# An FFT followed by two mixture-of-experts layers: an expert's last block moved to second place, with branch hints for TensorE

## The chip, the cores and the metric

The kernel runs on one core of a Trainium2 chip. The metric is the device time of one execution in microseconds (us). The core has five instruction streams: PE (TensorE, matmuls), DVE (VectorE), ACT (ScalarE), POOL (GpSimd) and SP (SyncE, which only issues DMAs). Each has its own sequencer, which the profile lists apart: it evaluates branches, loads registers and waits for semaphores.

## The reference

```
X = rfft(x, axis=1);  y = irfft(X * F)                 # 8 x 3072 tokens, 256 channels
x = y.reshape(24576, 256)
# first MoE: 8 experts, top 1
e = argmax(x @ w_gate);  g = softmax(x @ w_gate)[e]
out = g * sigmoid(x @ w_output_gate)[e] * (relu(x @ w1[e]) @ w2[e])     # 256 -> 1024 -> 256
# second MoE, top 1 with capacity 768: an expert takes its first 768 tokens, the rest give 0
e2 = argmax(out @ v_gate);  out2 = softmax(...)[e2] * (relu(out @ v1[e2]) @ v2[e2])
```

## The kernel before

Only the first 86 tiles of 128 tokens are worked on in the first round (`ROUNDS`); a second round follows only where the second MoE's experts aren't full by then (`k.full`, L1863). The FFT stage writes each token's row, by an indirect DMA, into the DRAM buffer `xs` at its expert's rows. The first MoE then takes each expert's rows in blocks. The matrix products run in three passes on rounded halves: a high part `_h` and a low part `_l` of the rows, of the weights and of the hidden values.

A plain block (`block1`, L1093) has 256 rows. Its first layer is four `l1_pair`s of 12 matmuls (L821 to L823); after each, ACT makes `h_h` (L826) and DVE `h_l` (L827). DVE also computes the logits of the second MoE for the block before (L1040, 16 a block). Then `prep` (L844) transposes the next block's rows on TensorE (L865), ACT copies out the high part and DVE the low part (L872). The second layer `l2` (L831) is twice 24 matmuls (L837 to L839); ACT scales the result into `x2` (L1140) and POOL scatters the rows (L1002) and the logits (L1020). A wide block (`block_wide`, L917) has 384 rows, with a first layer of 48 longer matmuls (L929 to L931) and a second layer of 72.

An expert's rows are cut by `cut_blocks` (L432) into a number of plain blocks, `k.plain`, and one last block, wide or narrow (256 rows), as `k.wide` says, from row `k.first` on. All counts are read into registers on every engine at run time.

`moe1` (L1189) goes through the eight experts. At the start of an expert SP loads the next expert's block 0 into buffer `b0` or `b1`, this expert's block 1 into `a1` (`load_x(e, 1)`), and the last block's rows into `xb_f` (`load_last`, L893). `load_x` (L874) takes its row from the table `k.ahead`, which repeats the last block's start where a block isn't there. Then comes block 0, which after its first layer prepares block 1 into `xt` and, between the halves of its second layer, the last block into `xt_f` (L851, L857, L858). ACT and POOL split the next expert's weights beside it (`next_w`, L794, L809, L810). Blocks 1 to 7 stand in seven nested conditions, `If(nb > j)` (L1211 to L1218); block j loads block j + 1 into `a0`, `a1` or `a2` by turns and prepares it, whether it is there or not. A branch that isn't taken leaves the whole nest, and each engine then brings its semaphores to where they would be had it gone through. After the nest comes `last_block` (L906) with the condition on `wide` (L911), the wide arm first; both arms prepare the next expert's block 0.

Expert 0 is special: its first four blocks are run by `head` (L1171) in the arm `early` (L712) of `one_round`, if enough of its rows were there before the last scatters; `late()` is the other arm, behind it in the code. In this data expert 0 has four plain blocks, all in that arm. Experts 0, 1, 2 and 6 have a narrow last block, 3, 4, 5 and 7 a wide one. After expert 7, the index work of the second MoE runs beside its last block, and `tile_kernel` (L1720) branches on `k.known` (L1849) into two forms of the second MoE's first blocks, the usual one first.

Of the kernel before, what the change touches and what calls it, by code (L numbers as in the profile page):

```python
# [431 lines left out]
def cut_blocks(k):  # L432
# [13 lines left out]
    nc.vector.tensor_copy(k.plain, k.cntf)  # L446
    STT(out=k.cntf, in0=k.cntf, scalar=256.0, in1=n, op0=ALU.mult, op1=ALU.subtract)
# [16 lines left out]
def one_round(k, r, cap):  # L464
# [46 lines left out]
    for bi, b in enumerate(batches):  # L511
# [68 lines left out]
        for q in range(NQ + 2):  # L580
# [19 lines left out]
            if nb is None and q == 8 and len(batches) > 1:  # L600
# [4 lines left out]
                with tc.If(early > 0):  # L605
                    moe.load_x(0, 0, True)
        j0, j1 = span[b]
# [54 lines left out]
    def aheads():  # L662
# [21 lines left out]
        )  # L684
        nc.vector.tensor_copy(k.ahead, k.aheadf)

    work = [gate.chain_a2, gate.chain_b, counts, pads, aheads, lambda: cut_blocks(k)]
# [20 lines left out]

    if early is None:
        late()  # L710
    else:
        with tc.If(early > 0) as c:  # L712
            for j in range(1, EARLY):
                moe.load_x(0, j, True)
            weights()
            run(last[0])
            moe.prep(*moe.rows(0, 0))
            moe.head(0, [(0, 1)], last[1:])
            nc.sync.dma_start(out=moe.w2gb, in_=k.a["w2gb"])
            beside = [work[:0], work[:0], work[:2], work[2:4], work[4:5], work[5:]]  # L720
            moe.head(1, [(0, 2)], [lambda f=f: run(*f) for f in beside], True)
            for j in range(2, EARLY - 1):
                moe.head(j, [(0, j + 1)])
            ahead()
            moe.load_x(0, EARLY)
            moe.head(EARLY - 1, [(0, None), (0, EARLY)])
        with c.Else():
            late()
# [5 lines left out]
class Moe:  # L734
# [15 lines left out]
    def alloc(self, p, px):  # L750
# [14 lines left out]
        k.pm = p.tile([128, 3, 8], F32, name="pm")  # L765
# [108 lines left out]
    def load_x(self, e, j, free=False):  # L874
# [3 lines left out]
        if j > 0 and not free:  # L878
# [4 lines left out]
                max_val=r0,  # L883
# [22 lines left out]
    def last_block(self, e, wide):  # L906

        s = e % 2
        final = e + 1 == E
        nxt = [] if final else [self.rows(e + 1, 0)]  # L910
        with self.tc.If(wide > 0) as c:  # L911
            self.block_wide(s, nxt, final)
        with c.Else():
            xt = [v[:, :, :256] for v in self.xtf]
            self.block1(s, self.xbf[:, :2, :], xt, 3, True, [], nxt, (), final)

    def block_wide(self, s, nxt, final):  # L917
# [23 lines left out]
        for rows, x in nxt:  # L941
            self.prep(rows, x)
# [235 lines left out]
    def head_late(self, nb, n):  # L1178
# [5 lines left out]
        for j in range(1, n):  # L1184
            with self.tc.If(nb > j):
                self.load_x(0, j + 1)
                self.head(j, [(0, j + 1)])

# [772 lines left out]
```

## Time and profile before

| what | before |
|---|---|
| median of 3 runs | 1326.87 us (1322.34 to 1327.99) |
| the profiled execution | 1321.05 us |
| its span, first to last instruction | 1319.3 us |
| mean granted TensorE clock | 0.961 |
| first MoE, blocks of experts 0 to 7 | from about 342 us to 992 us into the span |
| second MoE | from there on |

Times inside the profile are microseconds from the start of the span. A row of the waits says which engine and line waited for what: total us, how often, the longest. "issue" is time in which nothing that the profile shows was awaited. A name with a q (DVEq) is an engine's sequencer; the sequencer of TensorE is listed as PEldq. The granted clock is a share of 2.4 GHz: 1.00 is that level throughout a stretch, 0.50 is 1.2 GHz.

### The profile page before, as it was taken

The page shows a single profiled execution, that of the slowest core. Times are in us where ns is not written, and L with a number is a line of the kernel's source. Part 1 is how long each engine was busy: PE and PEld are TensorE (multiplying, and loading weights), DVE is VectorE, ACT ScalarE, POOL GpSimd, SP SyncE. Part 2 cuts the span into 40 slices and gives each one's busy share as a digit, 9 for nine tenths or more (in the row PEclk, how much of TensorE's full clock was granted, in tenths as well). Part 3 has the DMA queues.
Part 4 walks back from the last instruction along what each step waited for, and adds up shares of the span by engine and source line. Part 5 has one row for each costly group of instructions (what it writes and reads, how often), then busy time and mean ns, then how long its engine had stood idle before and what let it go on. Part 6 is the DMA issues. An engine that isn't in the chain of part 4 may idle for free. (4 is left out here: it accounts for less than half of the span.)

```text
span 1319.3 us, 25824 instructions
## 1 busy us (share of the span) xinstructions
PE 1207.2 (92%) x9338; PEld 1172.9 (89%) x9338; DVE 872.0 (66%) x2800; ACT 490.8 (37%) x872; POOL 557.2 (42%) x508
## 2 busy tenths in 40 slices
PE   6999999999885998989998899998997899999996
PEld 6899999989885998889898889988887899999996
DVE  3857676678473875867868688786857755555541
ACT  4363443633421422424233243332323344444431
POOL 0000160446262542634445273452635567676731
PEclk9999999999897999999999899998998999999998
DMA  9343280634563321513224051320512233333210
GB/s 259 123 139 115 63 276 1 204 128 137 185 178 103 108 80 31 165 44 126 70 67 141 27 159 51 117 89 28 157 41 79 66 106 112 97 99 105 71 46 22
DMA packets 85469, 138.95 MB, mean 105 GB/s; under 512 B 13463, under 2 KB 61339, under 8 KB 84889
## 3 DMA queue, kind: packets, MB, share of 16 engines
q1 hardware_dynamic: 61113, 71.07, 17.9%
q0 software_dynamic: 24144, 65.31, 15.5%
q8 instruction: 102, 1.67, 0.5%
q14 instruction: 110, 0.90, 0.2%
HBM read 78.02 MB, written 58.90 MB: 104 GB/s over the span
## 5 line engine op out<-in xcount | busy, mean ns | idle before, releaser
L827 DVE SCALAR_TENSOR_TENSOR h_l<-ps,h_h 128x512 fp32r<-128x512 f32 x252 | 173.4, 689 | 216.0 <-ACT h_h L826 214.4
L1040 DVE SCALAR_TENSOR_TENSOR junk<-x,w2gb 128x256 f32<-128x256 f32 x640 | 283.4, 494 | 0.0
L826 ACT ACTIVATE h_h<-ps 128x512 fp32r<-128x512 f32 x252 | 149.6, 598 | 211.9 <-PE ps L823 202.3
L1020 POOL DMA_INDIRECT lgtok<-lg,wtok x80 | 78.2, 978 | 254.3 <-DVE junk L1040 237.4
L400 POOL DMA_INDIRECT xs<-y,sli x86 | 87.8, 1021 | 214.9 <-DVE tt L234 115.4
L839 PE MATMUL ps<-w_0h,h_l 128*128 128x256 f32 x552 | 160.4, 291 | 17.0 <-DVE h_l L827 16.7
L839 PE MATMUL ps<-w_1h,h_l 128*128 128x256 f32 x552 | 159.9, 290 | 13.2 <-DVE h_l L827 13.1
L837 PE MATMUL ps<-w_0h,h_h 128*128 128x256 f32 x552 | 162.4, 294 | 0.0
L837 PE MATMUL ps<-w_1h,h_h 128*128 128x256 f32 x552 | 161.3, 292 | 0.0
L838 PE MATMUL ps<-w_0l,h_h 128*128 128x256 f32 x552 | 158.4, 287 | 0.0
L838 PE MATMUL ps<-w_1l,h_h 128*128 128x256 f32 x552 | 158.1, 286 | 0.0
L821 PE MATMUL ps<-xt_h,w_0h 128*128 128x256 f32 x480 | 137.4, 286 | 0.7 <-ACT xt_h L871 0.7
L822 PE MATMUL ps<-xt_l,w_0h 128*128 128x256 f32 x480 | 136.4, 284 | 0.2 <-DVE xt_l L872 0.2
L823 PE MATMUL ps<-xt_h,w_0l 128*128 128x256 f32 x480 | 136.3, 284 | 0.0
L821 PE MATMUL ps<-xt_h,w_1h 128*128 128x256 f32 x464 | 128.9, 278 | 1.6 <-ACT xt_h L871 1.6
L822 PE MATMUL ps<-xt_l,w_1h 128*128 128x256 f32 x464 | 128.8, 278 | 0.0
L823 PE MATMUL ps<-xt_h,w_1l 128*128 128x256 f32 x464 | 128.7, 277 | 0.0
L839 PEld LDWEIGHTS ps<-w_0h,h_l 128*128 128x128 f32 x552 | 107.9, 196 | 20.4 <-DVE h_l L827 20.4
L839 PEld LDWEIGHTS ps<-w_1h,h_l 128*128 128x128 f32 x552 | 107.8, 195 | 16.1 <-DVE h_l L827 15.8
L838 PEld LDWEIGHTS ps<-w_0l,h_h 128*128 128x128 f32 x552 | 108.2, 196 | 0.0
L837 PEld LDWEIGHTS ps<-w_0h,h_h 128*128 128x128 f32 x552 | 108.1, 196 | 0.0
L837 PEld LDWEIGHTS ps<-w_1h,h_h 128*128 128x128 f32 x552 | 107.9, 195 | 0.0
(288 smaller groups left out, 3058.1 us busy)
## 6 DMA issues: line engine op xcount, KB each, us to landing
out<-padrow SPq DMA_DIRECT2D x48, 512.0 KB, 6.4
raw<-v POOLq DMA_DIRECT2D x32, 512.0 KB, 4.2
raw<-w POOLq DMA_DIRECT2D x24, 512.0 KB, 4.4
xin<-x SPq DMA_DIRECT2D x40, 240.0 KB, 3.0
xb_a<-xs SPq DMA_DIRECT2D x35, 258.0 KB, 2.9
raw<-w SPq DMA_DIRECT2D x8, 512.0 KB, 5.9
f<-f SPq DMA_DIRECT2D x13, 256.0 KB, 4.6
xs<-padrow SPq DMA_DIRECT2D x8, 387.0 KB, 10.5
```

Source lines behind the costliest of these rows:

```text
L400: i = nc.gpsimd.indirect_dma_start(out=k.xs, out_offset=bass.IndirectOffsetOnAxis(ap=self.sli[:, j : j + 1], axis=0), in_=self.y[:, self.j ...
L821: nc.tensor.matmul(o, lhsT=wh[:, c, sl], rhs=xh[:, c, :], start=c == 0, stop=False)
L822: nc.tensor.matmul(o, lhsT=wh[:, c, sl], rhs=xl[:, c, :], start=False, stop=False)
L823: nc.tensor.matmul(o, lhsT=wl[:, c, sl], rhs=xh[:, c, :], start=False, stop=c == 1)
L826: nc.scalar.activation(hh, ps, AF.Relu)
L827: nc.vector.scalar_tensor_tensor(out=hl, in0=ps, scalar=0.0, in1=hh.bitcast(F32), op0=ALU.max, op1=ALU.subtract)
L837: nc.tensor.matmul(ps, lhsT=hh[:, f, sl], rhs=wh[:, f, :], start=f == 0, stop=False)
L838: nc.tensor.matmul(ps, lhsT=hh[:, f, sl], rhs=wl[:, f, :], start=False, stop=False)
L839: nc.tensor.matmul(ps, lhsT=hl[:, f, sl], rhs=wh[:, f, :], start=False, stop=f == 7)
L1020: i = nc.gpsimd.indirect_dma_start(out=k.lgtok, out_offset=bass.IndirectOffsetOnAxis(ap=tok, axis=0), in_=lg, in_offset=None, bounds_check ...
L1040: self.nc.vector.scalar_tensor_tensor(out=self.junk[:, n % 2, :], in0=x2, scalar=1.0, in1=self.w2gb[:, e, :], op0=ALU.mult, op1=ALU.mult, ...
```

## The change

In the experts 0 to 6 the last block now comes right after block 0 (after block 3 in expert 0), and the plain blocks from 1 on follow. No block prepares a block that isn't there: where block j is the last plain one, the table `k.ahead` now points `load_x(e, j + 1)` to the next expert's block 0, so that its rows are prepared in `xt` when the nest is left. The last block prepares nothing. Expert 7 keeps its order. TensorE gets branch hints (a register says which way the branch will go): for the `wide` branch ahead of block 0, for each `nb > j` one block ahead, for `early`, `known` and the skipped second round. The arms of `early` and `known` change places, so that the usual one is last in the code and ends without a jump. `cut_blocks` runs ahead of `aheads`, which needs the new tile `k.pend`, and the register loads of `wide` and `known` move to earlier places.

```diff
@@ cut_blocks
     nc.vector.tensor_copy(k.plain, k.cntf)
+    STT(out=k.pend, in0=k.cntf, scalar=256.0, in1=k.pm[:, 3, :], op0=ALU.mult, op1=ALU.add)
@@ one_round
                 early = nc.values_load(k.earlyi[0:1, 0:1], min_val=0, max_val=1)
                 with tc.If(early > 0):
                     moe.load_x(0, 0, True)
+                tc.mark_branch_hint_location("late", 1 - early, [mybir.EngineType.PE])
...
+        b3 = [128, 8, 8]
+        beyond = moe.beyond
+        nc.vector.tensor_tensor(
+            out=beyond,
+            in0=k.j256.unsqueeze(1).to_broadcast(b3),
+            in1=k.pend.unsqueeze(2).to_broadcast(b3),
+            op=ALU.is_ge,
+        )
+        nxt = k.pm[:, 4, :].unsqueeze(2).to_broadcast(b3)
+        nc.vector.tensor_tensor(out=moe.jump, in0=nxt, in1=k.aheadf, op=ALU.subtract)
+        nc.vector.tensor_tensor(out=moe.jump, in0=moe.jump, in1=beyond, op=ALU.mult)
+        nc.vector.tensor_tensor(out=k.aheadf, in0=k.aheadf, in1=moe.jump, op=ALU.add)
         nc.vector.tensor_copy(k.ahead, k.aheadf)
 
-    work = [gate.chain_a2, gate.chain_b, counts, pads, aheads, lambda: cut_blocks(k)]
+    work = [gate.chain_a2, gate.chain_b, counts, pads, lambda: cut_blocks(k), aheads]
...
-        with tc.If(early > 0) as c:
...
+        with tc.If(early < 1, label="late") as c:
+            late()
         with c.Else():
-            late()
+            soon()
@@ Moe
+    def hint(self, name, value=0):
+
+        label = f"{name}{self.k.rname}"
+        self.tc.mark_branch_hint_location(label, value, [mybir.EngineType.PE])
+
+    def more(self, nb, e, j):
+
+        self.hint(f"n{e}_{j}_", (nb - j + 63) >> 6)
+
-    def last_block(self, e, wide):
+    def last_block(self, e, wide, tell=lambda: None):
...
-        nxt = [] if final else [self.rows(e + 1, 0)]
-        with self.tc.If(wide > 0) as c:
-            self.block_wide(s, nxt, final)
+        with self.tc.If(wide > 0, label=f"w{e}_{self.k.rname}") as c:
+            tell()
+            self.block_wide(s, final)
         with c.Else():
+            tell()
             xt = [v[:, :, :256] for v in self.xtf]
-            self.block1(s, self.xbf[:, :2, :], xt, 3, True, [], nxt, (), final)
+            self.block1(s, self.xbf[:, :2, :], xt, 3, True, [], [], (), final)
@@ moe1
             if e == 0:
                 nb = nb0
+                wide = nc.values_load(k.wide[0:1, e : e + 1], min_val=0, max_val=1)
             else:
                 nb = nc.values_load(k.plain[0:1, e : e + 1], min_val=0, max_val=nxb)
+                wide = nc.values_load(k.wide[0:1, e : e + 1], min_val=0, max_val=1)
+                if final:
+                    self.more(nb, e, 1)
+                else:
+                    self.hint(f"w{e}_", wide)
                 self.load_x(e, 1)
                 self.load_last(e)
                 nxt = [self.rows(e, None), self.rows(e, 1)]
                 zero_out(k, ZFFT + (48 - ZFFT) * e // (E - 1))
                 self.block1(s, *self.bufs(e, 0), 0, True, self.extra(e), nxt)
-            wide = nc.values_load(k.wide[0:1, e : e + 1], min_val=0, max_val=1)
+            first = n0 if e == 0 else 1
+            if not final:
+                self.last_block(e, wide, lambda: self.more(nb, e, first))
             with ExitStack() as deep:
-                for j in range(n0 if e == 0 else 1, JU):
-                    deep.enter_context(tc.If(nb > j))
-                    nxt = []
+                for j in range(first, JU):
+                    deep.enter_context(tc.If(nb > j, label=f"n{e}_{j}_{k.rname}"))
                     if j + 1 < JU:
+                        self.more(nb, e, j + 1)
                         self.load_x(e, j + 1)
                         nxt = [self.rows(e, j + 1)]
+                    else:
+                        nxt = [] if final else [self.rows(e + 1, 0)]
                     self.block1(s, *self.bufs(e, j), 1 + j % 2, True, [], nxt)
...
-            if e + 1 == E and self.guess:
-                self.moe2_steps(0)
-            self.last_block(e, wide)
+            if final:
+                if self.guess:
+                    self.moe2_steps(0)
+                self.last_block(e, wide)
@@ tile_kernel
                         moe.go(LEAD[0])
+                        pre = nc.values_load(k.known[0:1, 0:1], min_val=0, max_val=1)
+                        tc.mark_branch_hint_location("known", 1 - pre, [mybir.EngineType.PE])
+                        moe.go(LEAD[1])
...
-                        with tc.If(pre > 0) as c:
+                        with tc.If(pre < 1, label="known") as c:
                             xg = dict(moe.xg)
-                            moe.moe2(0, n, BESIDE)
+                            moe.xg.clear()
+                            moe.go(LEAD[2])
+                            moe.moe2(0, n)
                         with c.Else():
                             moe.xg = xg
-                            moe.xg.clear()
-                            moe.go(LEAD[1])
-                            moe.moe2(0, n)
+                            moe.moe2(0, n, BESIDE)
...
-LEAD = ("KTUVXLWlMB01ax23yse", "bHPDGeomhctfKLsMBrX0123")
+LEAD = ("KTUVXLWl", "MB01ax23yse", "bHPDGeomhctfKLsMBrX0123")
```

## Rows read from the trace of the kernel before

**Rows 1.** The page, part 1: busy us (share of span), instructions.
```profile
PE 1207.2 (92%) x9338; PEld 1172.9 (89%) x9338; DVE 872.0 (66%) x2800; ACT 490.8 (37%) x872; POOL 557.2 (42%) x508
```

**Rows 2.** Waits of PE, whole span: us in total, times, longest.
```profile
PE ps L839 <- DVE h_l L827: 29.8, 22, 3.0
PE ps L821 <- issue: 25.3, 4, 10.2
...
PE ps L929 <- DVEq L1211: 3.7, 2, 1.9
```

**Rows 3.** Stretches of PE: us, busy (instructions), granted clock, DMA share, GB/s.
```profile
415.92:433.33 17.41, 7.17 (x51) 0.71 0.15 37
505.77:518.25 12.48, 7.31 (x50) 0.86 0.14 42
588.83:602.23 13.40, 8.63 (x50) 0.75 0.15 40
661.32:673.75 12.43, 10.16 (x50) 0.86 0.15 39
736.43:752.42 15.99, 11.01 (x50) 0.79 0.13 34
824.11:834.50 10.39, 8.62 (x50) 1.00 0.16 43
908.07:920.85 12.78, 7.66 (x50) 0.73 0.15 41
482.30:487.92 5.62, 5.62 (x52) 1.00 0.21 50
825.88:834.50 8.62, 8.62 (x50) 1.00 0.16 46
```

**Rows 4.** Branches: ns min/median/max, first and last start; L1211 at 503:508, L911 whole.
```profile
L1211 PEldq COMPARE_BRANCH  x2: 192/1844/3497, 503.5 to 507.2; - x2
L1211 DVEq COMPARE_BRANCH  x2: 47/55/63, 504.5 to 507.8; - x2
...
L911 PEldq COMPARE_BRANCH  x12: 85/296/3244, 422.8 to 991.7; - x12
```

**Rows 5.** POOL's catch-up (ns), SP's wait, its loads of `xb_a`, their landing.
```profile
L1211 POOLq INC_SWDGE_SEM  x8: 621/1336/2254, 422.4 to 972.5; - x8
...
SPq L886 <- DMA x2tok<-x,xb_a: 20.7, 1, 20.7
...
512.11 0.38 SPq L886 DMA_DIRECT2D xb_a<-xs  x1
...
914.90 0.38 SPq L886 DMA_DIRECT2D xb_a<-xs  x1
...
DMA to landing us min/median/max: 2.7/2.7/2.7
```

**Rows 6.** Timeline around expert 2's block after block 0, and that stretch of PE.
```profile
536.92 0.29 PE L821 MATMUL ps<-xt_h,w_0h 128*128 128x256 f32 x1
...
538.26 1.01 DVE L858 TENSOR_TENSOR xt_fl<-ps,xt_fh 128x384 fp32r<-128x384 f32 x2
...
540.45 0.69 DVE L827 SCALAR_TENSOR_TENSOR h_l<-ps,h_h 128x512 fp32r<-128x512 f32 x1 [0.89 <-ACT h_h L826]
...
545.03 2.67 DVE L1040 SCALAR_TENSOR_TENSOR junk<-x,w2gb 128x256 f32<-128x256 f32 x1
...
542.70:553.70 11.00, 8.10 (x54) 0.84 0.43 123
```

**Rows 7.** The chain (a set of transposes; issue time) and VectorE's timeline near 380.
```profile
1059.92 0.44 PE ps L865 x4
...
1052.96 0.96 issue
...
379.16 0.23 DVE L679 TENSOR_TENSOR aheadf<-aheadf,basec 128x64 f32<-128x64 f32 x1
...
387.96 0.17 DVE L1150 COPY ptok<-xb_a 128x2 int32<-128x2 int32 x1 [5.52 <-DMA lgtok<-lg,ptok]
```

More of the change, by code (lines that the diff above doesn't have):

```diff
@@ L707, in late, with soon @@
         moe.head_late(nb, EARLY)
+    def soon():
+        for j in range(1, EARLY):
+            moe.load_x(0, j, True)
+        weights()
+        run(last[0])
+        moe.prep(*moe.rows(0, 0))
+        moe.head(0, [(0, 1)], last[1:])
+        nc.sync.dma_start(out=moe.w2gb, in_=k.a["w2gb"])
+        beside = [work[:0], work[:0], work[:2], work[2:4], work[4:5], work[5:]]
+        moe.head(1, [(0, 2)], [lambda f=f: run(*f) for f in beside], True)
+        for j in range(2, EARLY - 1):
+            moe.head(j, [(0, j + 1)])
+        ahead()
+        moe.load_x(0, EARLY)
+        moe.head(EARLY - 1, [(0, None), (0, EARLY)])
     if early is None:
@@ L711, in one_round @@
     else:
-        with tc.If(early > 0) as c:
[L713 to L726, printed above, removed]
+        with tc.If(early < 1, label="late") as c:
+            late()
         with c.Else():
-            late()
+            soon()
     np = nc.values_load(k.plain[0:1, 0:1], min_val=0, max_val=k.R // 256)
@@ L764, in alloc @@
         )
-        k.pm = p.tile([128, 3, 8], F32, name="pm")
+        k.pm = p.tile([128, 5, 8], F32, name="pm")
+        k.pend = p.tile([128, 8], F32, name="pend")
+        self.beyond, self.jump = (p.tile([128, 8, 8], F32, name=n) for n in ("beyond", "jump"))
         nc.sync.dma_start(out=k.pm, in_=k.a["c_pm"])
@@ L940, in block_wide @@
                 g()
-        for rows, x in nxt:
-            self.prep(rows, x)
         if tail:
@@ L1187, in head_late @@
                 self.head(j, [(0, j + 1)])
+        self.load_x(0, n)
+        self.prep(*self.rows(0, n))
     def moe1(self, nb0, n0):
@@ L1230, in moe1 @@
                         self.block1(s, xb, xt, 3, True, [], [])
-            if e + 1 == E and self.guess:
-                self.moe2_steps(0)
-            self.last_block(e, wide)
+                    if not final:
+                        self.prep(*self.rows(e + 1, 0))
+            if final:
+                if self.guess:
+                    self.moe2_steps(0)
+                self.last_block(e, wide)
     def rank2(self, r):
@@ L1669, in moe2 @@
                 now, rest = now + rest, []
+            if self.k.rname == "r0" and n + 1 == len(seq):
+                full = nc.values_load(
+                    k.full[0:1, 0:1], engines=(mybir.EngineType.PE,), min_val=0, max_val=1
+                )
+                self.tc.mark_branch_hint_location("rest", 1 - full, [mybir.EngineType.PE])
             for q in range(4):
@@ L1863, in tile_kernel @@
                 k.fr = nc.values_load(k.full[0:1, 0:1], min_val=0, max_val=1)
-                with tc.If(k.fr < 1):
+                with tc.If(k.fr < 1, label="rest"):
                     body()
 ROUNDS = [(0, 86), (86, 192)]
-LEAD = ("KTUVXLWlMB01ax23yse", "bHPDGeomhctfKLsMBrX0123")
+LEAD = ("KTUVXLWl", "MB01ax23yse", "bHPDGeomhctfKLsMBrX0123")
 BESIDE = {
@@ L1896, in cut_consts @@
     least = np.array([EARLY] + [1] * (E - 1))
-    return np.stack([2 * least + 1, 2 * least + 3, least])
+    far = np.where(np.arange(E) == E - 1, 2.0**20, 0.0)
+    nxt = rows_per_expert() * np.minimum(np.arange(E) + 1, E - 1)
+    return np.stack([2 * least + 1, 2 * least + 3, least, far, nxt])
 def misc_consts(cap):
```

6 lines of the change are left out of this document (3 added, 3 removed).

## The prediction

> **What bounds it now.** I read the page's busy table first, then the waits of TensorE, then stretches of its busy time and clock, then the branches, and last the queues behind them. TensorE is busy for 92% of the span [rows 1], so little but its idle time can be won. Of that idle time two lines matter here. The first is waiting for `h_l` from VectorE; the second is "issue" ahead of the last block's first layer, where nothing in the data is awaited [rows 2]. In the order of before, that place is the end of an expert's plain blocks: TensorE stops at the end of the last plain block and takes up the last block some microseconds later. Seven stretches show it, each from the end of a plain block's second layer to the end of the last block's first layer [rows 3]. A clean first layer takes 5.62 us for 256 rows and 8.62 us for 384. Over that the seven lose 11.79, 6.86, 7.78, 3.81, 7.37, 1.77 and 7.16 us, for experts 0 to 6: 46.5 us together. Some of it is idle and some is the clock: the granted clock of these stretches is 0.71 to 0.86, that is a mix of the 2.4 and the 1.2 GHz level after the engine stood still, and 1.00 for expert 5, which stood only 1.77 us. Read as matmul time alone, the low clock costs 7.31 - 5.62 = 1.7 us (expert 1), 3.0 (2), 2.0 (6), 2.4 (4), and nothing in expert 5.
>
> What the idle time is stands in the branches of TensorE's sequencer [rows 4]. At expert 1 the branch out of the nest of plain blocks took 3.50 us, where the same branches elsewhere take 0.09 to 0.3, and the branch to the narrow arm took another 3.24 us. The first began at 503.5, 2.3 us before TensorE ran dry at 505.77. So the sequencer is about 2.3 us ahead of the engine: one far branch alone costs about 1.2 us, two in a row about 5. Expert 0 has three in a row, as it leaves the early arm as well.
>
> **The change, part by part.** *Branches.* With the hints working, the exits and the narrow arms cost about what a near branch costs. The last block moves between block 0 and the plain blocks, so that even unhinted branches no longer stand in a row. The hints themselves and their register arithmetic are sequencer work inside the 2.3 us of lead: nothing, and at worst 0.3 us a block, the length of a near branch, if the lead were gone. Expert 0 keeps one unhinted branch, into its narrow arm: 3.24 - 2.3 = 0.9 us with the whole lead, 3.24 with none, and the register loads of `plain` and `wide` now stand right ahead of it; I take 1.9 us.
>
> *What is late next.* Behind the nest now comes the next expert's block 0, and after its first layer TensorE transposes block 1, which SP loads at the start of the expert into buffer a1. The nest uses a1 too (j = 1, 4, 7), so this load waits until the nest is left on every engine. On POOL that takes the landing of the last scatters and then a semaphore catch-up of 0.6 to 2.3 us. Before, the same load already waited 20.7 us for the `x2tok` scatter, and was issued at 512.11, 6.34 us after the plain block's end at 505.77; the last of the six went out at 914.90, 6.83 us after 908.07. It landed 2.7 us after its issue [rows 5]. Before, that lay beside the whole last block. Now TensorE needs it 5.62 us after the plain block's end plus a tenth, and it lands after 9.0: a wait of 3.3 us at seven boundaries (into experts 1 to 7), 23.1 us. Below, the bound is 0 (a1 free when its last reader is done), above 6.83 + 2.7 - 5.7 = 3.8. I take 3.3, since the six issues are of this very load. The load of the last block's rows stands behind it on SP, and is needed half a second layer later: nothing. After such a wait the clock falls: 1.7 to 3.0 us where the pause was near 5, nothing at 1.77. I take 1.3 each, 9.1 us, bounds 0 and 3.0 each. VectorE also leaves the nest late (3.3 us between its two branches at expert 1 [rows 4], and TensorE waited for it twice, 3.7 us [rows 2]), but this lies inside the wait for the load.
>
> *Block 0 followed by the last block.* VectorE finishes the low part of the last block's transposed rows, `xt_fl`, at 539.27, while TensorE began the following block at 536.92 [rows 6]. Before, this was needed four blocks later; now it is needed at once. The wait would be up to 2.3 us in six experts; but TensorE's 3.3 us pause lets VectorE catch up first, and I take 0.4 each, 2.4 us. POOL's weight splits run at the same places as before: one logit took 2.67 us beside one, longer than the two halves of `xt_fl` together (1.01), and the block after block 0 loses its time to that (54 matmuls in 11.00 us, clock 0.84 [rows 6]). That stays. But VectorE's own branch into the narrow arm is not hinted. A far one costs it 3.3 us by the row of its two branches, against 0.89 us of slack ahead of its first `h_l` there [rows 4, 6]: 2.4 us where it is far, nothing where it is near. I take half, over three narrow experts 3.9 us (bounds 0 and 2.4 x 6).
>
> *Transposes.* One set per expert goes, 0.44 us [rows 7]. In six experts it lay ahead of a second layer which waits for `h_l` anyway, and the plain block that took that place now has it ahead of nothing: count them and the number outside the wait is the same. Only expert 0 gains, 0.4 us; bound 7 x 0.44 = 3.1.
>
> *The rest, at nothing.* The five new VectorE operations, near 0.23 us each, stand ahead of 5.52 us in which VectorE waits for a DMA [rows 7]; without that cover 1.2 us. Entering the early arm becomes a far branch for four engines without hints, in a place where TensorE waits for the first rows' DMA; bounds 0 and 3.3. In the second MoE the arm's end falls through, which takes away up to 0.96 us of "issue" [rows 7], and its start becomes a far branch for VectorE, which the chain runs through there: bounds -1 and +3.3, taken as nothing. The hint for the skipped second round acts after the work is done. The load of `known` moved ahead waits on a value that is there already when TensorE gets to it, with SP's, ACT's and POOL's later steps queued behind: nothing.
>
> **The sum.** New: 23.1 + 9.1 + 1.9 + 2.4 + 3.9 = 40.4 us against 46.5 now, and 0.4 for the transposes: 6.5 us less. The profiled execution took 1321.05 us, so 1314.6; the median of the runs, 1326.87, is 5.8 us above it, so by the runs **1320.4 us**. Its own range is 1312 to 1328.
>
> **Rivals.** *The load is in time.* Then its wait and most of the low clock are gone (32.2 us), but what lay inside it comes out: 2.0 us for `xt_fl` in six experts, 12, and 1.85 us for VectorE's exit at four boundaries, 7.4. Left are 12 + 7.4 + 1.9 + 3.9 = 25.2 us against 46.5, with the transposes 21.7 less: 1305.2. For it: only the deep arms that are skipped make the wait. Against: all six issues came together with POOL's catch-up. Chance 0.17.
>
> *VectorE's own code is what is late.* Place: the branch on `wide`, between block 0 and the last block, unhinted on VectorE. Price: 2.4 us in all six experts, and 0.8 us more of low clock behind the longer wait (3.0 against some 2 us after shorter ones), 19.2 us in place of 3.9: 1335.7, slower than before. It decides from 1.1 us per expert beyond what I counted. For it: the wait there is already VectorE's, 29.8 us in all [rows 2], and the idle time before the last block in which it caught up is gone. Against: where branch and target lie close, nothing is paid. Chance 0.20.
>
> *The hints do nothing.* The exit then costs 3.50 - 2.3 = 1.2 us, which the wait for the load covers; the narrow arm costs 0.9 us in three experts, 2.7 together: 1323.1. Against it speaks nothing in the rows, as no hinted branch is among them. Chance 0.15. The Trainium skill, Runtime: NRT & Kernel Launch, section on instruction fetch mechanics, says that code is prefetched only in sequence, and that a taken branch out of the window stalls for a fetch; by that rule the hints would change nothing. The far branches above agree with its second half; no row bears on the first.
>
> **How the numbers follow.** The forecast has the remaining 0.48. About 0.5% of the time, 6.6 us, is what a measurement of this kernel can tell from no change, and the forecast lies almost on that line: half of it (0.24), the early load (0.17) and a little of the rival without hints (0.04) are faster by more, 0.45. The other half, 0.09 of the rival without hints and a little of the VectorE one lie within it, 0.34. The rest is slower, 0.21. The range for 8 in 10 runs from below the early load's 1305 to the VectorE rival's 1336, with the unknown clock cost in it: 1302 to 1336.
>
> **What would show it.** In the profile after: exits of the nest on TensorE at about 0.1 to 0.3 us instead of 3.5 (hints right); a new wait of TensorE's transposes for the DMA into `xb_a`, seven times near 3.3 us (my main term); SP's issue of that load still about 6.3 us after a plain block's end; the last block's wait for `h_l` no longer than now. No such DMA wait, and the early load is right. A longer wait for `h_l` in the last block, with VectorE starting late in it, and the second rival is. If "issue" stays ahead of the plain or the last blocks, the hints fail.

## The result, and the profile after

The changed kernel takes 1287.82 us (median of 4 runs, 1283.69 to 1288.69) where the kernel before takes 1326.13 us on the same chip: 0.9709 of it, 95% interval 0.9678 to 0.9739. It is **faster by 38 us**; 1320.4 us were forecast, and the result lies outside the range. The profiled execution took 1283.69 us, its span is 1281.9 us, 37.4 us less than before, and the mean granted clock is 0.978. TensorE's busy time fell by 16.5 us although its work is nearly the same (28 instructions fewer): it ran at the lower clock less often [rows 1].

From the page and the waits of TensorE over the whole span (us in total, times, longest us):

```profile
PE 1190.7 (93%) x9310; PEld 1156.1 (90%) x9310; DVE 866.9 (68%) x2798; ACT 490.4 (38%) x865; POOL 560.2 (44%) x508
...
PE ps L858 <- DVE h_l L846: 11.8, 8, 4.5
PE ps L884 <- DMA xb_a<-xs: 8.8, 7, 3.1
PE ps L840 <- ACTq L1249: 7.9, 6, 1.4
...
PE ps L884 <- DMA xb_b<-xs: 4.3, 1, 4.3
PE ps L959 <- DVE xt_fl L877: 4.2, 3, 1.6
PE ps L1493 <- DVE xt_l L891: 4.1, 1, 4.1
```

Against [rows 2], nothing is left of the 25.3 us of "issue" ahead of the narrow last blocks, as forecast; the one row of "issue" that TensorE still has there, 2.2 us, stands ahead of expert 4's block 0. But 18.0 of the 29.8 us of waiting for `h_l` went too, which the forecast had left where they were. What came instead, the waits for the load into `xb_a`, for the exit of the other engines (ACTq L1249) and for `xt_fl`, comes in short waits, 1.4 to 3.1 us at the longest.

TensorE's branches, by line (ns min/median/max, first and last start), the plain blocks' line first before and then after, and the last blocks' after:

```profile
L1211 PEldq COMPARE_BRANCH  x39: 65/70/4252, 418.4 to 969.4; - x39
...
L1249 PEldq COMPARE_BRANCH  x39: 65/70/1483, 427.0 to 926.9; - x39
...
L938 PEldq COMPARE_BRANCH  x12: 65/308/4132, 416.6 to 951.2; - x12
```

Each line has 39 branches and only eight of them are exits. These took 3.4 to 4.25 us before; now seven take 0.34 to 0.37 us and one 1.48. Of the branches into the last blocks one is still long, expert 6's with 4.13 us; TensorE then starts that block 2.3 us late.

The new boundary, from the end of an expert's last plain block (in expert 0, of its narrow last block) to the start of the second layer of the next expert's block 0, in stretches of TensorE (us, busy, granted clock, DMA share, GB/s):

```profile
429.24:439.29 10.05, 6.41 (x54) 1.00 0.22 55
507.61:516.00 8.39, 6.43 (x54) 1.00 0.29 67
585.88:595.23 9.35, 6.40 (x53) 1.00 0.27 63
656.09:666.25 10.16, 7.83 (x52) 0.83 0.22 53
727.58:735.58 8.00, 6.40 (x53) 1.00 0.27 71
808.45:817.96 9.51, 7.88 (x52) 0.82 0.26 55
886.72:895.69 8.97, 6.13 (x53) 1.00 0.29 65
sum 64.43, PE 47.49; mean PE 6.78
```

A clean one takes 5.62 us for the layer and 0.44 for the transposes [rows 3, 7], so the seven lose 64.43 - 42.4 = 22.0 us. The places they replace lost 46.5.

The other half of the gain is in the block after block 0. The same view of seven such blocks, from first layer to first layer, of experts 1 to 7; first the kernel before, where it is a plain block of 11.66 us without losses:

```profile
452.11:470.45 18.34, 13.92 (x103) 0.91 0.42 125
...
939.62:956.28 16.66, 13.77 (x103) 0.90 0.45 135
sum 117.84, PE 95.47; mean PE 13.64
```

and the changed kernel, where it is the last block (narrow, narrow, three wide, narrow, and expert 7's plain one):

```profile
447.26:460.84 13.58, 11.97 (x98) 1.00 0.43 137
522.40:538.83 16.43, 13.76 (x99) 0.90 0.48 153
601.70:620.97 19.27, 17.90 (x122) 1.00 0.45 144
672.63:692.34 19.71, 17.68 (x123) 1.00 0.43 133
742.05:761.67 19.62, 17.90 (x122) 1.00 0.42 134
826.88:839.74 12.86, 11.73 (x97) 1.00 0.43 135
902.17:914.52 12.35, 12.04 (x103) 1.00 0.52 168
sum 113.82, PE 102.98; mean PE 14.71
```

How long these would be without a loss is measured below (e5 and e6): 11.69 us for the plain block, 11.40 for the narrow one, which prepares nothing, 16.95 for the wide, 11.92 for expert 7's. So before lost 117.84 - 81.85 = 36.0 us here, and the changed kernel 113.82 - 97.0 = 16.9: 19.1 us gained.

Expert 7 shows how. Its order of blocks did not change, and yet its block after block 0 fell from 16.66 to 12.35 us. The timeline of POOL and VectorE at the end of that block's first layer, with the row of TensorE that waits for the last `h_l`, before:

```profile
947.07 0.68 DVE L827 SCALAR_TENSOR_TENSOR h_l<-ps,h_h 128x512 fp32r<-128x512 f32 x1
947.67 2.67 DVE L1040 SCALAR_TENSOR_TENSOR junk<-x,w2gb 128x256 f32<-128x256 f32 x1
947.68 2.37 POOL L810 TENSOR_TENSOR w_0l<-raw,w_0h 128x1024 fp32r<-128x1024 f32 x1
...
950.62 0.68 DVE L827 SCALAR_TENSOR_TENSOR h_l<-ps,h_h 128x512 fp32r<-128x512 f32 x1
...
951.36 0.58 PE L839 MATMUL ps<-w_1h,h_l 128*128 128x256 f32 x1 [2.58 <-DVE h_l L827]
```

and after:

```profile
910.34 0.68 DVE L846 SCALAR_TENSOR_TENSOR h_l<-ps,h_h 128x512 fp32r<-128x512 f32 x1
910.43 1.00 POOL L1029 DMA_INDIRECT x2tok<-x,xb_b  x1 [2.14 <-issue]
...
911.07 0.39 PE L858 MATMUL ps<-w_1h,h_l 128*128 128x256 f32 x1 [0.31 <-DVE h_l L846]
...
911.45 2.41 POOL L829 TENSOR_TENSOR w_0l<-raw,w_0h 128x1024 fp32r<-128x1024 f32 x1
911.54 2.62 DVE L1067 SCALAR_TENSOR_TENSOR junk<-x,w2gb 128x256 f32<-128x256 f32 x1
```

Both times POOL's fourth subtraction of the weights stretches the logit beside it, 0.41 us elsewhere, to 2.6 or 2.7 us. Before, that logit stands ahead of the block's last `h_l`, so TensorE pauses for 2.58 us, and its clock is down in that stretch (0.90). After, POOL stood 2.14 us for nothing that the profile shows, the subtraction fell behind the last `h_l` (910.34), and nobody waited for the logit. In a wide last block the same subtraction lies beside a first layer that is 3 us longer, with its last `h_l` due 3 us later: in expert 3's the logit at 609.21 takes 2.81 us ahead of the `h_l` at 611.96, and TensorE waits for no `h_l` there. The wide ones lose 2.3 to 2.8 us, of which 1.2 to 1.6 are a wait for `xt_fl`; the narrow ones still lose 1.5 to 5.0.

The Trainium skill, SBUF — State Buffer, section on the two separate sides, says that VectorE and GpSimd arbitrate for one pair of ports, and that a VectorE operation with two SBUF inputs is fully blocked while a GpSimd operation that reads SBUF holds it. The rows agree: the logit reads two tiles and ends 0.3 us behind the subtraction in both timelines (though before, the two start within 0.01 us, which does not tell which came first), while `h_l`, which reads PSUM and one tile, keeps its 0.69 us beside it (at 904.99 in the changed kernel, inside a subtraction that began at 904.77).

### The profile page after: what moved, and what is told of

It reads as the page before. It is cut to its first block, busy times and chain, and to the rows that moved or that the text cites. A ratio compares the mean times of both kernels' runs of the same rounds, so it can differ in the third digit from the quotient of the medians.

```text
span 1281.9 us, 25783 instructions
## 1 busy us (share of the span) xinstructions
PE 1190.7 (93%) x9310; PEld 1156.1 (90%) x9310; DVE 866.9 (68%) x2798; ACT 490.4 (38%) x865; POOL 560.2 (44%) x508
## 5 line engine op out<-in xcount | busy, mean ns | idle before, releaser
L1067 DVE SCALAR_TENSOR_TENSOR junk<-x,w2gb 128x256 f32<-128x256 f32 x640 | 280.6, 490 | 0.0
L858 PE MATMUL ps<-w_0h,h_l 128*128 128x256 f32 x552 | 157.1, 285 | 10.4 <-DVE h_l L846 9.9
L856 PE MATMUL ps<-w_0h,h_h 128*128 128x256 f32 x552 | 159.4, 289 | 0.0
L858 PEld LDWEIGHTS ps<-w_0h,h_l 128*128 128x128 f32 x552 | 105.3, 191 | 12.3 <-DVE h_l L846 11.4
L857 PEld LDWEIGHTS ps<-w_1l,h_h 128*128 128x128 f32 x552 | 106.5, 193 | 0.0
L857 PEld LDWEIGHTS ps<-w_0l,h_h 128*128 128x128 f32 x552 | 105.5, 191 | 0.0
```

Source lines behind the costliest of these rows:

```text
L856: nc.tensor.matmul(ps, lhsT=hh[:, f, sl], rhs=wh[:, f, :], start=f == 0, stop=False)
L857: nc.tensor.matmul(ps, lhsT=hh[:, f, sl], rhs=wl[:, f, :], start=False, stop=False)
L858: nc.tensor.matmul(ps, lhsT=hl[:, f, sl], rhs=wh[:, f, :], start=False, stop=f == 7)
L1067: self.nc.vector.scalar_tensor_tensor(out=self.junk[:, n % 2, :], in0=x2, scalar=1.0, in1=self.w2gb[:, e, :], op0=ALU.mult, op1=ALU.mult, ...
```

## The experiments

Every run was timed beside the kernel before on the same chip. e1 to e4 share one chip and e13 to e16 another, on which before takes 1324 and 1325 us. e5 to e8 and e9 to e12 went to two slower chips, on which it takes 1394 and 1395; by the profiles most of the 70 us more lie ahead of expert 0's last block (61 us there between e12 and e2). Across chips ratios to before are compared, and for e5 to e8 with e9, the changed kernel on the other slow chip.

**The hints and the orders apart.** e1 takes all hints out of the changed kernel; e2 puts those of seven exits into the kernel before.

```diff
 def hint(self, name, value=0):
-    self.tc.mark_branch_hint_location(label, value, [mybir.EngineType.PE])
+    return
...      # and the hints for early, known and the second round
```

> The changed kernel with every hint taken out; the new order of blocks and arms stays. Theory A (the hints end TensorE's stalls at far branches, and this is most of the gain): TensorE waits some 3.4 us again at about 12 branches (eight exits from the plain blocks, the narrow arms of four experts). At the seven exits that lead to block 0 some 2.7 of it counts, since block 0 starts 1.3 us late today in any case and waits 0.8 us for its load, together 7 x 2 = 14 us; the last expert's exit costs nothing more, VectorE's own exit being as late; four narrow arms 4 x 3.2 = 13 us; some us of lower clock on top: about 1316 us. Theory B (the new order of the blocks brings the gain, since the POOL engine's weight splits fall elsewhere, and the hints do nothing): about 1289 us, and the branches in the trace are as short as now.

```diff
 # kernel before, moe1
+                self.more(nb, e, 1)
                 self.load_x(e, 1)
...
-                    deep.enter_context(tc.If(nb > j))
+                    deep.enter_context(tc.If(nb > j, label=f"n{e}_{j}_{k.rname}"))
+                        self.more(nb, e, j + 1)
```

> The kernel before, in its old order, with one thing of the change: a hint for TensorE a block ahead of each exit from the plain blocks of experts 1 to 7. Theory A (hints work in any order): TensorE's 3.5 us at seven exits fall to 0.2 us; the next wait is VectorE's exit from the same blocks, which ends some 2 us after TensorE's branch begins, so about 1.5 us are left over at each: 7 x 2 = 14 us gained, and a little clock: about 1309 us. Theory B (the order is what counts, the hints do nothing): 1326 us.

e1 took 1291.04 us, 0.9742 of before (0.9705 to 0.9779); e2 1307.14 us, 0.9863 (0.9819 to 0.9907). So the new order alone brings 33 us, the hints alone 17, both 38. For e1 neither theory holds: the time is near B's, but the branches aren't. TensorE's branches in e1:

```profile
L936 PEldq COMPARE_BRANCH  x12: 65/296/459, 416.4 to 962.4; - x12
...
L1247 PEldq COMPARE_BRANCH  x39: 65/70/3842, 426.8 to 936.9; - x39
```

The exits take 3.3 to 3.8 us again. But the branch into the narrow arm, 3.24 us at most before [rows 4], takes at most 0.46 us **without any hint**, now that a block and not another far branch stands ahead of it. My theory A had charged 13 us for it. That what stands ahead is the cause is not shown: in e2 the narrow arms without hints, behind an exit that has become short, take 0.84, 1.01 and once 3.47 us. And the seven boundaries of e1, same stretches as above:

```profile
429.10:440.06 10.96, 6.12 (x52) 1.00 0.20 50
508.27:518.28 10.01, 7.62 (x54) 0.83 0.30 63
...
sum 73.28, PE 53.00; mean PE 7.57
```

lose 73.28 - 64.43 = 8.9 us more than with hints: 1.3 us each and not 3.4, since with hints TensorE waits there for ScalarE's exit and for the load instead. Its pauses are 2.3 to 3.0 us without hints, and the clock is down (0.71 to 0.84) in six of the seven stretches, where with hints it is in two. Between the medians it is 3 us, and the intervals overlap. In e2 theory A held to 2 us.

**The arms, and VectorE's branches.** e3 gives `early` and `known` their old order of arms, hints kept; e4 gives the hints of `hint()` to VectorE too.

```diff
-        with tc.If(early < 1, label="late") as c:
-            late()
+        with tc.If(early > 0, label="late") as c:
+            soon()
...      # known likewise; both hints turned round
```

> The changed kernel with the likely arms first again (the early arm and the known arm), hints kept. Theory A (the new order of the arms costs as much as it gives, since the engines without hints branch far into the likely arm): the first block of the early arm starts 3.3 us sooner, the wait of 4.1 us for xt_l in the known arm goes, and in exchange TensorE leaves the two arms by a far branch of 3.6 us each, of which some 2 to 3.6 us count: 1288 - 7.4 + 6 = about 1287 us, no difference. Theory B (the arms are part of the gain, TensorE's far branches out of them being worth more): 1292 us or more. Theory C (only the entry counts, the exits being hidden behind other engines): 1281 us.

```diff
-        self.tc.mark_branch_hint_location(label, value, [mybir.EngineType.PE])
+        self.tc.mark_branch_hint_location(label, value, [mybir.EngineType.PE, mybir.EngineType.DVE])
```

> The changed kernel with the same hints (the exits and the arms of the last block) given to VectorE as well as to TensorE. Theory A (after TensorE, VectorE's own exit is the wait at each boundary): block 0 begins 1.3 us sooner at seven places, and the last expert's exit loses its wait of 2.9 us: up to 12 us gained, 1276 us. Theory B (the load of block 1, issued by SP only after its own exit, is right behind: TensorE then waits for xb_a instead): only the last expert's 2.9 us and some 0.3 us at each boundary: 1283 us. Theory C (hints on VectorE cost it time at each block or do nothing): 1288 us or more.

e3: 1290.06 us, 0.9742 (0.9696 to 0.9788), no difference to the changed kernel; between A and B the run can't decide. The first block starts 3.7 us sooner (343.11 against 346.77), but this is not the arms' doing by what the runs show: 1.9 of it are there in the FFT stage already, and in e15, which has the old order of arms, that block starts at 347.46. What does come with the old arms is 5.5 us of "issue" behind the early arm's end; what goes is the 4.1 us wait for `xt_l` (0.5 in e3). e4: 1283.62 us, 0.9689 (0.9653 to 0.9724), where B put it, but the interval overlaps the changed kernel's, and B's reason failed: the wait at expert 7's exit is still 3.2 us (2.9 without these hints). At the seven boundaries the waits for VectorE's exit, 1.2 us, are nearly gone (0.25), and those for `xb_a` grew from 5.7 to 9.5 us: the load takes over what VectorE gives.

**POOL's subtractions.** e5 and e6 leave out the low parts of the weights of experts 2 to 7 and of the second MoE's first one, in the kernel before and in the changed one.

```diff
-        eng.tensor_tensor(out=lo, in0=raw, in1=hi.bitcast(F32), op=ALU.subtract)
+        if g < 2 or g > 8:
+            eng.tensor_tensor(out=lo, in0=raw, in1=hi.bitcast(F32), op=ALU.subtract)
```

> The kernel before without the low parts of the weights of experts 2 to 7 and of the second MoE's first expert: the POOL engine's subtraction is left out (four of 2.4 us in each block 0 of experts 1 to 7), so these outputs lack that part; ScalarE's copies and the loads stay. Theory A (the block after block 0 lost its 5 us to these subtractions, beside which a VectorE logit takes 1.8 to 2.9 us): the block after block 0 falls from 16.7 to about 12 us, seven times: 1324 - 33 = about 1291 us. Theory B (the block after block 0 is late for another reason, TensorE's own order or its clock): 1320 us or more.

> The changed kernel with the same subtractions left out (the same parts of the output are missing). Theory A (the new order took some 18 of the 36 us that the POOL engine's subtractions cost, the wide last blocks and the later fourth subtraction covering the rest): what is left of them is the loss of the block after block 0, 17.7 us, and the waits for xt_fl in it: 1288 - 16 = about 1272 us, and the difference between the two orders without subtractions is under 20 us. Theory B (the gain of the new order comes from the branches and the clock alone): the difference between the orders stays some 36 us, 1255 us.

e5: 0.9741 of before (0.9678 to 0.9803), 35 us less; e6: 0.9639 (0.9591 to 0.9687), against 0.9816 for the changed kernel in e9. The block after block 0 in e5:

```profile
521.85:533.51 11.66, 11.66 (x103) 1.00 0.54 173
...
sum 81.85, PE 81.85; mean PE 11.69
```

TensorE has no idle time left in these blocks and a clock of 1.00: all 36.0 us there were POOL's. In e6, a narrow, a wide and expert 7's block, which give the clean times used above (three of the other four agree to 0.1 us; expert 6's took 12.79 us at a clock of 0.88, behind the pause at its long branch; TensorE waits for `xt_fl` in none):

```profile
506.83:518.24 11.41, 11.41 (x98) 1.00 0.59 196
661.48:678.43 16.95, 16.95 (x122) 1.00 0.30 98
962.87:974.79 11.92, 11.85 (x103) 1.00 0.64 225
```

Theory A holds in both: without subtractions the orders are 16 us apart (1358.75 and 1342.84), not 36. That e6 lies 25 us below e9 by the ratios, rather than 16, is not explained by the blocks alone.

**Moving the subtractions, the preparations, the loads.** e7 lets VectorE compute the low parts; e8 swaps the two loads and preparations of block 0; e9 is the changed kernel itself; e10 issues the loads of block 1 and the last block an expert ahead, into buffers of their own; e11 joins e10, e7 and e4; e12 is e2 with e7's edit.

```diff
 # e7, extra
-        eng = self.nc.vector if e == 0 else None
+        eng = self.nc.vector
 # e8, moe1, experts 1 to 6
-                self.load_x(e, 1)
                 self.load_last(e)
-                nxt = [self.rows(e, None), self.rows(e, 1)]
+                self.load_x(e, 1)
+                nxt = [self.rows(e, 1), self.rows(e, None)]
 # e10, moe1, start of expert e (tiles xb_f1, xb_c0 added)
+            self.xbf = self.xbfs[e % 2]
+            if e < E - 1:
+                self.load_x(e + 1, 1)
+                self.load_last(e + 1)
```

> The changed kernel with the low parts of all experts' weights computed by VectorE (1.22 us each in block 0 of expert 0) instead of POOL (2.42 us each). Theory A (a subtraction on POOL costs VectorE 1.4 to 2.2 us at the logit beside it, more than the 1.22 us that it takes on VectorE itself): 4 x 0.6 us less delay in seven blocks, of which about half comes before the last block's second layer: about 1280 us. Theory B (VectorE's queue then waits for ScalarE's copy ahead of each subtraction, and h_l comes later): 1290 us or more.

> The changed kernel with the two loads and the two preparations of block 0 swapped for experts 1 to 6: the last block's rows are loaded first and transposed ahead of block 0's second layer, block 1's rows between the halves of that layer. Theory A (the waits for xb_a, 8.8 us in all, and for xt_fl, 5.8 us, come from the load behind the exit and from the last block's rows being prepared late): the xt_fl waits go, and the wait for the load stays, now for xb_f, which is half as large again: about 1283 us. Theory B (the wait for xt_fl is VectorE's lateness and shows up at h_l instead, and the larger load adds 0.5 us at each boundary): 1288 to 1292 us.

> The changed kernel itself, once more, as the yardstick for the three beside it on this chip: 0.97 of the kernel before.

> The changed kernel with the loads of block 1 and of the last block of expert e+1 issued at the start of expert e, into buffers of their own (a second tile for the last block, one more for block 1), so that neither lies behind the exit from the plain blocks. Nothing else is changed. Theory A (at each boundary TensorE loses about 1.3 us to the exits of the other engines and 0.8 us to the load that SP issues after its exit; one follows the other): the waits for xb_a of 8.8 us in all go, six or seven times 0.8 to 1.3 us, and the clock has one gap fewer: 0.994 of the changed kernel, 1280 us where that is 1288. Theory B (the load hides behind what comes late anyhow: without it TensorE waits for VectorE's h_l or xt_fl): no difference to the changed kernel.

> The kernel with the loads ahead, VectorE computing the low parts of the weights in place of POOL, and the hints given to VectorE too. Theory A (the three are losses of their own: 8 us for the loads, some 8 us for POOL's subtractions in the last blocks, 4 us for VectorE's exits): 0.985 of the changed kernel, about 1268 us where that is 1288. Theory B (they hide one another): 0.994, as with the loads alone.

> The kernel before in its old order of blocks, with the hints at its seven exits and with VectorE computing the low parts of the weights: neither the new order of the blocks nor that of the arms. Theory A (the order of the blocks helps only because POOL's subtractions fall elsewhere in it): 1324 - 17 for the hints - 25 for the block after block 0 = 1282 us, as fast as the changed kernel or faster, 0.965 to 0.975 of before. Theory B (the order has a gain of its own at the exits): 1297 us or more, 0.98 of before.

| run | ratio to before | 95% interval |
|---|---|---|
| e7 | 0.9653 | 0.9604 to 0.9702 |
| e8 | 0.9781 | 0.9723 to 0.9839 |
| e9, the changed kernel | 0.9816 | 0.9760 to 0.9872 |
| e10 | 0.9816 | 0.9749 to 0.9884 |
| e11 | 0.9591 | 0.9523 to 0.9660 |
| e12 | 0.9800 | 0.9741 to 0.9859 |

e9 misses its 0.97: the change brings 25 us on this slower chip, not 38, and why is not settled (its seven experts, from expert 1's block 0 on, took 549.2 us against 526.7). e8 and e10 show no difference to e9, as theory B has it, but their intervals reach 8 to 9 us to either side, so the 5 to 8 us of the theories A are not excluded. In e10's trace no wait for `xb_a` is left at the boundaries (4.2 us in e9's), and its median is 3.9 us lower: the load whose wait was my main term is worth nothing that can be measured here. VectorE's subtractions are worth some 23 us (e7 against e9, 0.9653 and 0.9816, on two chips), three times what A said, and e11 as much with some 10 us on top, more than A; what of the 10 is the loads ahead and what VectorE's hints, no run tells. e12 is as fast as the changed kernel, which speaks for A, but its number is B's; the next runs ask it again without hints.

**Order against subtractions.** On a chip as fast as the first: e13 takes the arms' hints out of the changed kernel, e15 and e16 give VectorE the subtractions in the old order and in the new order without hints, and e14 joins the parts that helped.

```diff
 # e13
-                else:
-                    self.hint(f"w{e}_", wide)
 # e15 (kernel before), e16 (e1), extra
-        eng = self.nc.vector if e == 0 else None
+        eng = self.nc.vector
 # e14: e11 and e13, and in moe1
-                nb = nc.values_load(k.plain[0:1, e : e + 1], min_val=0, max_val=nxb)
-                wide = nc.values_load(k.wide[0:1, e : e + 1], min_val=0, max_val=1)
+                nb, wide = soon      # both read by expert e - 1, ahead of its last block
```

> The changed kernel without the hints for the last block's arms; the hints of the exits, of the early and known arms and of the second round stay. Theory A (these hints do nothing for six experts, since the branch takes 0.4 us without one in the new order, and cost one: expert 6's branch takes 4.13 us with it): the wait of 2.3 us ahead of expert 6's last block and its slower clock go: 0.997 of the changed kernel, 1284 us where that is 1288, and no branch into a last block over 0.5 us. Theory B (the hints do serve the narrow arms): three branches of some 3 us come back: 1295 us.

> The kernel with the loads ahead and VectorE computing the low parts, without the hints for the last block's arms, and with each expert's two counts read into the engines' registers ahead of the exit instead of after it (TensorE spends 0.9 us on the two reads and the hint between its exit and block 0). Theory A (the exit's own 2 us at each boundary are partly these reads): 7 x 0.8 us and expert 6's 3 us less than the kernel with the loads ahead and VectorE: 0.966 of the changed kernel. Theory B (ScalarE's and VectorE's exits are later than TensorE's reads, so only expert 6's 3 us go): 0.973 of the changed kernel.

> The kernel before with one edit: VectorE computes the low parts of the weights in place of POOL. Theory A (the block after block 0 lost its time to POOL's subtractions): that block falls from 16.7 to some 12.5 us in seven experts: 0.978 of before. Theory B (a subtraction on VectorE costs as much as POOL's did): 1.0 of before.

> The changed kernel without any hint (the new order alone) and with VectorE computing the low parts. Theory A (of the order's 33 us some 19 come from POOL's subtractions, which cost the last block less than the plain block, and some 11 from four branches into the narrow arm): without POOL's subtractions the new order is 10 to 15 us faster than the old one with the same edit, not 33. Theory B (the order's gain is at the exits and arms alone): it stays over 25 us faster. Theory C (it is POOL's subtractions alone): the two are within 5 us.

| without hints | POOL subtracts | VectorE subtracts |
|---|---|---|
| old order | 1324.82 (before) | 1288.73, 0.9722 (0.9662 to 0.9782) |
| new order | 1291.04, 0.9742 (e1) | 1274.68, 0.9617 (0.9572 to 0.9662) |

(e1 was timed beside before at 1323.97 us.) This tells what the order gains: 33 us with POOL's subtractions, 14 without (within theory A's 10 to 15; the two intervals touch, so C's under 5 us is only just out). The 14 can be found in the traces: TensorE's waits ahead of e15's last blocks of experts 0 to 6 are 35.0 us together, those ahead of e16's next blocks 0 17.2, and waits for `xt_fl` in e16 take 5.0 back. POOL's subtractions cost the old order 36 us more than VectorE's, the new one some 16. One edit of one line in the old order does as much as the whole change. In e15 the logits (L1040) and the block after block 0:

```profile
L1040 DVE SCALAR_TENSOR_TENSOR junk<-x,w2gb x640: 408/415/480, 392.9 to 936.8; 128x256 f32<-128x256 f32 x160
...
L810 DVE TENSOR_TENSOR w_0l<-raw,w_0h x20: 1209/1216/1226, 327.6 to 916.6; 128x1024 fp32r<-128x1024 f32 x20
```

```profile
456.89:469.17 12.28, 11.97 (x102) 1.00 0.56 175
...
sum 86.50, PE 84.33; mean PE 12.05
```

No logit takes over 0.48 us (3.03 us at most in the changed kernel); a subtraction takes VectorE 1.22 us, and the seven blocks lose 86.50 - 81.85 = 4.7 us in place of 36.0.

e13: 1284.51 us, 0.9685 (0.9634 to 0.9736), the time of A, but its reason fell: expert 6's branch takes 5.06 us without its hint too. The other branches into last blocks stay short, so these hints do nothing, and B is out. Why that one branch is long with the exits' hints (e13, e4) and 0.36 us without any (e1) stays open.

e14 took **1255.43 us, 0.9485 (0.9442 to 0.9529)**, faster than both kernels. It is 0.977 of the changed one, short of what either theory said, and no more than e11 reached against e9; so what the counts read ahead bring by themselves is not shown. Its first six boundaries and its blocks after block 0:

```profile
429.77:437.64 7.87, 6.39 (x53) 1.00 0.08 23
...
sum 44.26, PE 37.24; mean PE 6.21
```

```profile
444.94:457.05 12.11, 11.95 (x96) 1.00 0.76 256
...
sum 102.38, PE 99.10; mean PE 14.16
```

The six boundaries lose 44.26 - 36.4 = 7.9 us, against 19.1 for the same six of the changed kernel (the seventh takes 7.9 us against 9.0), and the clock stays at 1.00; the blocks take 102.38 us against 113.82.

## Why the prediction was wrong

The mechanism at the exits was right and three terms were wrong in size; one sentence about a part that I took as untouched was wrong in kind. In the order of the prediction:

- *"With the hints working, the exits and the narrow arms cost about what a near branch costs"*: so it is, except for expert 6. But the remark beside it, that unhinted branches no longer stand in a row, fits e1, where the narrow arms cost nothing without any hint, and I drew no number from it. Expert 0's 1.9 us for its unhinted arm are nothing: 0.35 us, no wait.
- *The load, 23.1 us.* SP's issue is near where I put it, 4.9 to 7.0 us behind the plain block's end, 6.3 forecast; at expert 2, whose boundary begins at 507.61, it is 5.1:

```profile
512.75 0.39 SPq L905 DMA_DIRECT2D xb_a<-xs  x1
```

  TensorE's waits for it are 8.8 us, of which one of 3.1 belongs to expert 0's blocks: 5.7 at the seven boundaries. One step that failed is "this lies inside the wait for the load": ScalarE's and VectorE's exits come before it. TensorE starts block 0 1.1 to 2.2 us late, and so needs the load that much later. One pause of 3.3 us was forecast; one of 1.1 to 2.2 us came ahead of block 0 and a second of up to 2.0 at the load, and after most of them the clock stayed at 1.00.
- *The low clock, 9.1 us*: it fell in two of seven boundaries, 7.83 and 7.88 against some 6.4 us of busy time, 2.9 us. So the boundaries cost 22.0 us and not 32.2; in e10, with the load out of the way, the pauses at the exits stay, 1.4 to 2.4 us each.
- *`xt_fl` 2.4 us, VectorE's narrow arm 3.9*: TensorE waited 4.2 us for `xt_fl` in the wide arms and 1.6 in the narrow ones, about the sum of both. That the sums agree is luck: most of it came in the wide arms, where I had put 1.2 of the 6.3, and none of it is left in e6, so the subtractions are behind it and not VectorE's branch. (Half of 2.4 over three experts is 3.6, not 3.9.)
- *"the block after block 0 loses its time to that"*, and *"That stays."* **This is the step that failed most.** The cause was read rightly (36.0 us, all of it POOL's, e5 and e15), but that it would cost another block as much was assumed. Its cost hangs on whether the stretched logit stands ahead of a `h_l` that TensorE needs. Against a longer first layer, or a subtraction 2 us later, all of it together cost 16.9, the waits for `xt_fl` included. In the prediction's terms 36.0 + 2.4 + 3.9 = 42.3 became 16.9: this is 25 of the 31 us by which the gain was missed, and the boundaries are 10.
- *The rest at nothing*: the early arm's first block begins 3.3 us later (346.77 against 343.49), the upper bound I gave for a far branch, but no branch is shown to do it: TensorE is 1.7 us behind in the FFT stage already, SP issues the load that is waited for (`xb_b`, 4.3 us) at 342.06, ahead of its branch into the arm at 343.14, and e15 with the old arms begins that block as late, behind a wait of 4.2 us for the same load. The chain in the second MoE waits 4.1 us for VectorE's `xt_l` behind its branch into the `known` arm (0.5 before), and from expert 7's last block on the kernel loses 3.0 us, near the upper bound of 3.3. With the arm in the same place this wait is 0.5 to 0.8 us in e4, e14 and e16; why it differs stays open.

Together: 46.5 - 22.0 at the exits, 19.1 in the block after block 0, less 3.3 and 3.0, is 37.3 us, and the span fell by 37.4. That it agrees to a tenth is luck: terms of up to 2.3 us of both signs (the wait ahead of expert 6's last block, those in expert 0's blocks) cancel. Of the rivals, the load in time (1305.2) came nearest, and a part of it came about: the load's wait and the low clock fell to 5.7 and 2.9 us, and the exits of the other engines, which had been hidden behind it in the sum, became the first wait. But half of the gain is in none of them. "The hints do nothing" is refuted by the branches and by e2. The Trainium skill, Runtime: NRT & Kernel Launch, section on instruction fetch mechanics, has code prefetched in sequence alone; here the exits take 0.34 to 0.37 us and once 1.48 with hints, and 3.3 to 3.8 without (e1), so the rows differ from that rule. In the new order the hints are worth 9 us at the boundaries by the profiles and 3 by the medians, whose intervals overlap, because the next engine's exit and the load stand 1 to 2 us behind TensorE's own.

## What to carry to other kernels

Where an engine is slowed by another's operation beside it (a row whose longest time is seven times its median), price that operation by what stands behind the slowed one, and ask for every edit of order where it falls now; then try to move it to the slowed engine itself, which here was worth as much as the whole change. A branch hint, a load ahead or a faster exit on one engine is worth only the distance to the next late engine: list the exits of all engines and the loads behind them before adding up one engine's stalls.

## What the runs showed of the hardware

- POOL needs 2.42 us for the subtraction of two 128x1024 tiles that VectorE does in 1.22, and a VectorE operation that reads two tiles, 0.41 us alone, took up to 3.03 us beside it (the changed kernel, L1067), while `h_l`, which reads PSUM and one tile, kept its 0.69 us.
- The branch of TensorE into a narrow arm takes, without a hint, 0.35 to 0.46 us when a block stands ahead of it (e1; in e16 two of four took 1.0 and 1.4, and expert 6's in e13 5.06) and 2.7 to 3.4 when it follows another far branch (before, e15); behind a hinted exit it took 0.8 to 1.0 and once 3.5 (e2). The exit from the nested conditions takes 3.3 to 4.3 without a hint (before, e1, e15).
- Which pauses of TensorE bring its clock down is not settled: in the changed kernel a stretch with pauses of 1.3 and 0.3 us has 0.82 (808.45), one with pauses of 1.1, 0.6 and 2.0 us 1.00 (429.24).
- Two of the chips ran the kernel before 70 us slower than the others; on the one where the changed kernel was timed, the change brought 25 us instead of 38.
